# A fused attention and MLP-mixer kernel: another order for its first stage

## The chip, the cores and the metric

The kernel runs on one core of one Trainium2 chip. The time is device time in microseconds (us) of one execution, as the median over several runs. A separate execution is recorded by the hardware profiler; its span runs from the first to the last instruction of the program, and its own time is a little longer than its span, because starting and ending the program lie around it.

The engines are TensorE (PE, matrix products; PEld is its loading of the stationary operand), VectorE (DVE), ScalarE (ACT), GpSimd (POOL) and SyncE (SP), which here issues nearly all loads. Each engine works through its own instructions strictly in the order of the program, and semaphores make it wait for others.

## The reference

Attention without a softmax, for 8 batches of 8 heads, 576 tokens and 64 columns a head, with a root-mean-square normalisation, and then a token and channel mixer on 576 tokens of 512 columns:

```python
kv  = einsum('bhsd,bhse->bhde', k, v)
out = einsum('bhsd,bhde->bhse', q, kv)
rms = sqrt(mean(out * out, axis=-1, keepdims=True) + 1e-6)
x   = out / rms * g_norm                  # heads side by side: (8, 576, 512)
h   = maximum(x.T @ w_tok1, 0) @ w_tok2   # w_tok1 576x256, w_tok2 256x576
u   = x + h.T
out = u + maximum(u @ w_ch1, 0) @ w_ch2   # w_ch1 512x1536, w_ch2 1536x512
```

q, k, v and `g_norm` are float32. The four mixer weights arrive as float64, so the kernel loads their raw 64-bit words and turns them into float32 itself.

## The kernel before

**Tiling.** Batches are taken in pairs. The 576 tokens of a batch are four tiles of 128 rows and a rest of 64; the rests of the two batches of a pair share one tile. For each pair the kernel forms `kv` from k and v (two loads of k and two of v for each batch, half of the columns each), multiplies q by it, normalises, and mixes over tokens. The channel mixer over all batches follows in products of 128x256 and 128x128 blocks, and makes up most of the run. The stage that concerns us is the first: attention of pair 0 (batches 0 and 1), and the first half of its token mixing.

**The order of the work** is written out by hand. Near the end of the main function stand calls that issue loads, and then lists of short names; `play` (line 1192) takes the names one by one and emits the instructions of each. The list of the first stage is `start` (line 1241), the list after it `middle` (line 1247), which works on pair 1's attention and the rest of pair 0's mixing. The names that matter, with a tile number c (0 to 4, where 0 and 1 belong to batch 0, 2 and 3 to batch 1, and 4 is the rest) and a half t of it (128 rows each):

- `kvSH`: k transposed times v on TensorE for batch S, half H of the columns, into a PSUM tile; `eSH` copies it to SBUF as `kvp` (VectorE, line 383, in this stage). `lSH` issues the loads of k and v of the next pair into the same buffers.
- `aCT`: q times `kvp` on TensorE into a PSUM tile `ps_o`, of which there are two. `gCT` multiplies it by `g_norm` into the tile `x` (VectorE, line 444), `qCT` squares it (ScalarE, line 448), `tCT` sums the squares by head (VectorE, line 465).
- `mC`, `rC`, `iC`: mean (VectorE), square root (ScalarE), and a refined reciprocal (four VectorE instructions, lines 479 to 484), for a tile's 256 rows at once.
- The scaling of `x` by the result: `pCT` on GpSimd (`scale_pool`, line 504), `dCT` on VectorE (`scale_vector`, line 500) or `sCT` on ScalarE (line 498, eight instructions).
- `wBK`: turning block B of the raw token weights into float32. `wB0` issues the load; `wB1` is two ScalarE instructions (lines 163 and 166), `wB2`, `wB3`, `wB4` are three of VectorE (lines 169, 173, 178), in that order. Blocks 0 and 1 are the two halves of the columns of `w_tok1`, 2 its last 64 rows, 3 and 4 are `w_tok2`.
- `h0TJ`: the product of row tile J of batch 0's `x` with column block T of `w_tok1`, one matmul of 128x128 by 128x512 into the tile `ps_h` of block T. `h1T` is four such products, of batch 1's `x`.
- `jN`: N matmuls of an identity matrix with itself, whose result nobody reads (`keep_warm`, line 1277).

**Queues.** A load is issued by SP, but v of the first two loads by ScalarE. Loads share eight semaphores in turn, so a load waits until the one eight before it has landed. `load(n)` (line 138) is a load of k and v, `load_q(b)` one of q for a batch, `block[0]()` the load of a raw weight block. Before `start` the order is: `load(0)`, raw blocks 0 and 1, `load(1)`, q of batch 0, `load(2)`, `load(3)`, q of batch 1, and so on.

**Waits by range.** A wait is derived from the range of a tile that an instruction touches, from its first to its last element. `w_tok1` is laid out as rows by 256 columns, so that column blocks 0 and 1 alternate in each partition.

Of the kernel before, what the change touches and what calls it, by code (L numbers as in the profile page):

```python
# [20 lines left out]
def kernel(  # L21
# [90 lines left out]
    def do(f, *a, **kw):  # L112
        return lambda: f(*a, **kw)
# [6 lines left out]
    def dma(o, i, engine=nc.sync):  # L120
        keep(engine.dma_start(o, i))
# [16 lines left out]
    def load(n):  # L138

        if n >= 2 * B:  # L140
            return
        cols = [t[n // 2, :, ts(n % 2, DH)] for t in (k, v)]

        queues = (nc.sync, nc.scalar if n < 2 else nc.sync)
        for dst, c, e in zip((k_in[n % 4], v_in[n % 4]), cols, queues):
            dma(dst[:, :J], c[:LO].rearrange("(j p) e -> p j e", p=P), e)
            dma(dst[:HF, J], c[LO:], e)

    def load_q(b):
        if b < B:  # L150
            qT[b] = qtp.tile([P, HP, LO], F32, name="qT", tag="qT", bufs=2)
            dma(qT[b], q[b].rearrange("(c p) s -> p c s", p=P)[..., :LO])
# [69 lines left out]
    def get_ch2(f):  # L222

        a = 2 * (2 * f // NS)

        def loads(raw):
            t = raw.rearrange("p (h f n) w -> p f h n w", h=2, f=2)
            rows = words(moe_w_ch2)[ts(f, 2 * P)].rearrange("(f p) (h n) w -> f p h n w", f=2, h=2)
            return [(t[:, i], rows[i]) for i in range(2)]

        dst = w_ch2[:, a:a + 2, ds(2 * f % NS, 2)]
        return block(2 * DM, loads, dst.rearrange("p h f n -> p h (f n)"))
# [19 lines left out]
    def t_sums(b):  # L252

        def step(o, x, y):
            return lambda: tensor_add(b(o), b(x), b(y), ALU.subtract)

        return [step(5, 7, 1), step(6, 3, 5), step(7, 3, 7), step(4, 2, 6)]
# [934 lines left out]
    def play(lines, after={}, **stages):  # L1192

        for name in " ".join(lines).split():
            if name.isdigit():
                for _ in range(int(name)):
                    next(stages["rounding"], lambda: None)()
            elif name[0] == "-":  # L1200
                stages["before"][name[1:]]()
            else:
                next(stages[s][name] for s in ("attention", "mixing", "more")
                     if name in stages.get(s, ()))()
# [4 lines left out]
    channel = ([get_ch1(c, f) for f in range(2) for c in range(NC)]  # L1209
               + [get_ch2(f) for f in range(NF // 2)])  # L1210
    load(0)
    for block in tok1[:2]:
        block[0]()
    load(1)
    for t in [t for pair in zip(k_in, v_in) for t in pair]:
        keep(nc.gpsimd.memset(t[HF:, J], 0.0))
    zeroed = [ps["kv"].tile([P, 2, P], F32, name="ps_kv", tag="kv") for _ in range(2)]
    for t in zeroed:
# [5 lines left out]
    make_identity(nc, ident)  # L1224
    dma(g_sb, bass.AP(tensor=g_norm.tensor, offset=g_norm.offset,
                      ap=[[0, P], [0, 1], list(g_norm.ap[0])]), nc.scalar)
    load_q(0)
    for n in range(2, 4):
        load(n)
    load_q(1)  # L1230
# [2 lines left out]
    for block in tok1[2:] + tok2:  # L1233
# [5 lines left out]


    start = [
        "kv00 e00 l00 j14 w01 w11 w02 w03 w04 w12 w13 w14", "kv01 j10 e01 l01",
        "a00 g00 q00", "a01 g01 q01 t00", "a10 g10 q10 t01 m0 r0", "a11 g11 q11 t10 i0 p00 p01",
        "kv10 j6 t11 m1 r1 e10 i1 s10 p11", "kv11 j2 e11", "h000 h001 h002 h003", "a20 g20 q20", "a21 g21 q21 t20",
        "h010 t21 m2 r2", "a30 g30 q30 i2 p20", "a31 g31 q31 t30", "h011 t31 m3 r3 p21", "a40 i3 p30 g40 q40 p31",
        "h012 h013 t40 m4 r4 w21 i4 s40 lq0 l10 l11 lr0 lr1"]
    middle = [
        "kv00 e00 w31 w22 w23 w24", "h10 -lq1 w32 w33 w34", "kv01 e01 w41 w42",
        "h11 w43 w44", "hr l00", "a0 q00 g01 q01 g00 t00 t01", "u0 z2 f0", "u1 l01",
# [20 lines left out]
    more = {f"w{n}{k}": f for n, b in enumerate(tok1 + tok2) for k, f in enumerate(b)}  # L1270
# [6 lines left out]
    def keep_warm(n):  # L1277

        o = ps["h"].tile([P, DM], F32, name="ps_j", tag="h")
        for _ in range(n):  # L1280
            matmul(o[:, :P], lhsT=ident, rhs=ident, start=True, stop=True)

    more |= {f"j{n}": do(keep_warm, n) for n in (2, 6, 10, 14)}
    play(start, attention=attentions[0], mixing=mixings[0], more=more)
    play(middle, attention=attentions[1], mixing=mixings[0], before=attentions[0],
         more=more, rounding=rounding)
    for n in range(1, B // 2 - 1):
        play(steady[n - 1], attention=attentions[n + 1], mixing=mixings[n], before=attentions[n],
             more=more, rounding=rounding)
# [16 lines left out]
    more = {f"c{i}": f for i, f in enumerate(t_sums(lambda n: uT[0][:, SB[n]]))}  # L1306
# [97 lines left out]
```

## Time and profile before

| What | Value |
|---|---|
| Time, median of 3 runs | 789.48 us (788.86 to 789.51) |
| The profiled execution's own time | 788.88 us |
| Its span | 787.1 us |
| PE busy in the span | 774.4 us, 98% |
| VectorE, ScalarE, GpSimd busy | 612.9, 265.4, 78.3 us |
| First matmul starts | 6.24 us |
| First matmul of `middle` starts | 39.79 us |
| DMA from 2 to 79 us | busy throughout, 327 to 351 GB/s by stretch |

A fixed share of time lies outside the span: 788.88 - 787.1 = 1.8 us. TensorE's busy time counts the `jN` matmuls too, and matmuls at a lower clock at their longer duration. In the timeline, a 128x128 float32 matmul is shown as two records, and the `xN` at a line's end counts records.

### The profile page before, as it was taken

The numbers are of one execution on the slowest core, as the hardware profiler recorded it, in microseconds if no ns is written. First come the engines' busy times: TensorE is split into PE (matmuls) and PEld (weight loads), VectorE is DVE, ScalarE is ACT, GpSimd is POOL, SyncE is SP. The second block draws the span as 40 slices with busy tenths as digits, with TensorE's granted clock in tenths as the row PEclk, the third lists the DMA queues.
The fourth block names the chain that finished last, engine by engine and source line by source line (L and its number), as shares of the span: only waits on it lengthen the run. The fifth ranks groups of instructions, "written<-read, shape, count | busy, mean of one in ns | idle before, by whom it ended". The sixth has DMA issues, their size and how long they took to land.

```text
span 787.1 us, 14853 instructions
## 1 busy us (share of the span) xinstructions
PE 774.4 (98%) x5832; PEld 652.6 (83%) x5832; DVE 612.9 (78%) x906; ACT 265.4 (34%) x513; POOL 78.3 (10%) x91
## 2 busy tenths in 40 slices
PE   6999999999999999999999999999999999999998
PEld 5655555544888888999988899998889999889998
DVE  2666887796776868988778889776898885787977
ACT  2356564846110133511133242123352113325211
POOL 1211212122410000010100001010000101000111
PEclk9999999999999999999999999999999999999999
DMA  9999999587699795599897579889559889655864
GB/s 295 327 334 371 361 371 344 212 268 282 235 292 337 269 339 148 154 309 205 246 236 231 151 218 272 247 203 290 148 158 283 206 222 230 200 153 151 200 173 91
DMA packets 132614, 192.12 MB, mean 244 GB/s; under 512 B 13633, under 2 KB 92225, under 8 KB 132545
## 3 DMA queue, kind: packets, MB, share of 16 engines
q1 hardware_dynamic: 115984, 167.54, 68.1%
q0 software_dynamic: 14656, 22.02, 13.7%
q10 hardware_dynamic: 1904, 1.61, 0.7%
q8 instruction: 46, 0.75, 0.4%
q14 instruction: 24, 0.19, 0.1%
HBM read 138.31 MB, written 52.82 MB: 243 GB/s over the span
## 4 chain that ended last, share of the span: by engine, by line
PE 95%; DVE 2%; ACT 1%; DMA 1%; issue 0%; SPq 0%; ACTq 0%
PE ps_d L133 28%; PE ps_b L133 19%; PE ps_a L133 19%; PE ps_h L133 8%; PE ps_u L133 8%; PE ps_v L133 5%; PE ps_c L133 3%; PE ps_kv L133 2%; PE ps_w L133 2%; PE ps_o L133 2%; DMA raw<-in_moe_w_tok_dram 1%; ACT x L498 1%; DVE x L444 0%; DVE ms L465 0%; PE ps_j L133 0%
## 5 line engine op out<-in xcount | busy, mean ns | idle before, releaser
L133 PE MATMUL ps_d<-ui,w 128*128 128x256 f32 x504 | 118.6, 379 | 0.0
L133 PEld LDWEIGHTS ps_d<-ui,w 128*128 128x128 f32 x504 | 95.1, 190 | 12.8 <-DVE v L124 0.2
L130 ACT COPY ps_d<-ps_a 128x768 f32<-128x768 f32 (+1 forms) x56 | 32.0, 571 | 215.6 <-PE ps_a L133 215.6
L124 DVE TENSOR_TENSOR v<-v,v 128x1536 f32<-128x1536 f32 (+2 forms) x70 | 103.5, 1483 | 0.3
L133 PE MATMUL ps_b<-w,sv 128*128 128x128 f32 x672 | 84.7, 276 | 0.0
L133 PE MATMUL ps_a<-w,v 128*128 128x128 f32 x672 | 84.2, 275 | 0.0
L133 PEld LDWEIGHTS ps_a<-w,v 128*128 128x128 f32 x672 | 79.9, 192 | 0.2
L133 PEld LDWEIGHTS ps_b<-w,sv 128*128 128x128 f32 x672 | 79.5, 192 | 0.2
L133 PE MATMUL ps_u<-h,w_tok 128*128 128x512 f32 (+1 forms) x160 | 67.2, 606 | 0.2
L133 PE MATMUL ps_d<-w,v 128*128 128x128 f32 x528 | 66.3, 275 | 0.0
L133 PE MATMUL ps_h<-x,w_tok 128*128 128x512 f32 (+1 forms) x160 | 65.5, 603 | 0.7 <-ACT x L498 0.7
L133 PEld LDWEIGHTS ps_d<-w,v 128*128 128x128 f32 x528 | 62.7, 192 | 0.3
L127 ACT ACTIVATE v<-v 128x768 f32<-128x768 f32 (+1 forms) x54 | 42.6, 821 | 55.1 <-DVE v L124 55.1
L133 PE MATMUL ps_d<-w,sv 128*128 128x128 f32 x480 | 60.1, 275 | 0.0
L133 PEld LDWEIGHTS ps_d<-w,sv 128*128 128x128 f32 x480 | 57.1, 192 | 0.2
L133 PEld LDWEIGHTS ps_h<-x,w_tok 128*128 128x128 f32 (+1 forms) x160 | 26.1, 189 | 32.7 <-issue 29.0
L1121 POOL DMA_DIRECT2D out_dram<-us x11 | 14.1, 1278 | 379.3 <-ACT us L130 347.4
L133 PEld LDWEIGHTS ps_u<-h,w_tok 128*128 128x128 f32 (+1 forms) x160 | 24.8, 179 | 31.0 <-issue 25.6
L133 PE MATMUL ps_a<-uT,w 128*128 128x256 f32 x192 | 46.7, 379 | 0.0
L444 DVE TENSOR_TENSOR x<-ps_o,g_sb 128x512 f32<-128x512 f32 x32 | 21.6, 687 | 28.6 <-PE ps_o L133 23.3
L133 PE MATMUL ps_b<-ui,w 128*128 128x256 f32 x168 | 40.8, 379 | 0.0
L133 PEld LDWEIGHTS ps_a<-uT,w 128*128 128x128 f32 x192 | 36.3, 190 | 4.8
(145 smaller groups left out, 1216.2 us busy)
## 6 DMA issues: line engine op xcount, KB each, us to landing
w<-parts SPq DMA_DIRECT2D x168, 384.0 KB, 4.1
w<-parts SPq DMA_DIRECT2D x56, 192.0 KB, 3.4
uT<-blocks SPq DMA_DIRECT2D x36, 256.0 KB, 5.7
k_in<-in_k_dram SPq DMA_DIRECT2D x16, 512.0 KB, 8.7
qT<-in_q_dram SPq DMA_DIRECT2D x8, 1024.0 KB, 9.2
out_dram<-x POOLq DMA_DIRECT2D x16, 512.0 KB, 6.1
v_in<-in_v_dram SPq DMA_DIRECT2D x14, 512.0 KB, 8.8
raw<-in_moe_w_ch_dram SPq DMA_DIRECT2D x8, 768.0 KB, 10.4
```

The lines of the kernel that those rows point to most:

```text
L124: keep(engine.tensor_tensor(out=o, in0=a, in1=b, op=op))
L127: keep(nc.scalar.activation(o, a, AF.Relu))
L130: keep(nc.scalar.copy(o, a))
L133: keep(nc.tensor.matmul(*a, **kw))
L444: keep(nc.vector.tensor_mul(x, bank[c, h], g_sb.to_broadcast([P, number(c), D])))
L498: keep(nc.scalar.activation(x[:, k, h], x[:, k, h], AF.Copy, scale=inv[:, k, h]))
L1121: keep(nc.gpsimd.dma_start(to.rearrange("t p e -> p t e"), a, accum_op=ALU.add))
```

## The change

In the order of loads, `load(1)` and q of batch 0 go ahead of the raw token weights. In `start`, a long row of identity matmuls comes first, the weights are decoded between the steps of tiles 0 and 1, the `kv` products of batch 1 come between token-mixing products of batch 0, and all scaling that GpSimd did is given to VectorE or ScalarE (`p00 p01 p11 p20 p21 p30 p31` go; of them `d00 d01 d20 d30` are VectorE's and `s11 s21 s31` ScalarE's; `s10` becomes `d10` and `s40` becomes `d40`). The identity matmuls were 14, 10, 6 and 2, and are 24, 8 and 10.

```diff
     load(0)
+    load(1)
+    load_q(0)
     for block in tok1[:2]:
         block[0]()
-    load(1)
...
-    load_q(0)
     for n in range(2, 4):
         load(n)
...
     start = [
-        "kv00 e00 l00 j14 w01 w11 w02 w03 w04 w12 w13 w14", "kv01 j10 e01 l01",
-        "a00 g00 q00", "a01 g01 q01 t00", "a10 g10 q10 t01 m0 r0", "a11 g11 q11 t10 i0 p00 p01",
-        "kv10 j6 t11 m1 r1 e10 i1 s10 p11", "kv11 j2 e11", "h000 h001 h002 h003", "a20 g20 q20", "a21 g21 q21 t20",
-        "h010 t21 m2 r2", "a30 g30 q30 i2 p20", "a31 g31 q31 t30", "h011 t31 m3 r3 p21", "a40 i3 p30 g40 q40 p31",
-        "h012 h013 t40 m4 r4 w21 i4 s40 lq0 l10 l11 lr0 lr1"]
+        "j24 kv00 e00 l00 j8", "kv01 e01 l01", "a00 g00 q00", "a01 g01 q01 t00 t01 m0 w01 r0 w02 w03",
+        "a10 i0 d00 w04 d01 g10 q10 w11", "a11 w12 w13 g11 q11 w14 j10", "h000 h001 t10 t11 m1 r1", "kv10 e10 i1 d10 s11",
+        "h010 h011 kv11 e11", "a20 g20 q20", "a21 g21 q21 t20 t21 m2 r2", "h002 h012", "a30 g30 q30 i2 d20 s21",
+        "h003 h013", "a31 g31 q31 t30 t31 m3 r3", "a40 g40 q40 i3 d30 s31 t40 m4 r4 w21 i4 d40 lq0 l10 l11 lr0 lr1"]
...
-    more |= {f"j{n}": do(keep_warm, n) for n in (2, 6, 10, 14)}
+    more |= {f"j{n}": do(keep_warm, n) for n in (8, 10, 24)}
```

## The prediction

> **What bounds the kernel now.** I read the page first, for the engine that carries the span.
>
> ```profile
> span 787.1 us, 14853 instructions
> ...
> PE 774.4 (98%) x5832; PEld 652.6 (83%) x5832; DVE 612.9 (78%) x906; ACT 265.4 (34%) x513; POOL 78.3 (10%) x91
> ...
> PE 95%; DVE 2%; ACT 1%; DMA 1%; issue 0%; SPq 0%; ACTq 0%
> ```
>
> TensorE is the bound; other engines can stand on the path only where it idles. So second I read whom TensorE waits for:
>
> ```profile
> PE ps_kv L133 <- DMA v_in<-in_v_dram: 6.2, 1, 6.2
> PE ps_kv L133 <- DVE w_tok L178: 1.1, 1, 1.1
> PE ps_o L133 <- ACT sq L448: 0.8, 2, 0.5
> PE ps_h L133 <- ACT x L498: 0.7, 1, 0.7
> PE ps_r L133 <- ACT sq L448: 0.2, 1, 0.2
> ```
>
> Nearly all waits lie before 37 us: asked from 52 us on, the list holds one of 0.2 us. Hence **a delay in the first stage has nothing later to hide in, and a gain nothing that eats it**, as long as loads keep up. (The second row names a decode step; the load of k that this product needs was issued at 6.16 and landed 7.5 us later, at 13.7, when it started. That load is what came last.) Third, TensorE's timeline of the stage:
>
> ```profile
> 6.24 2.40 PE L133 MATMUL ps_kv<-v_in,k_in 128*64 128x64 f32 x40 [6.24 <-DMA v_in<-in_v_dram]
> 8.57 4.07 PE L133 MATMUL ps_j<-ident 128*128 128x128 f32 x28
> 13.77 1.39 PE L133 MATMUL ps_kv<-v_in,k_in 128*64 128x64 f32 x40 [1.14 <-DVE w_tok L178]
> 15.09 2.50 PE L133 MATMUL ps_j<-ident 128*128 128x128 f32 x20
> 17.42 1.95 PE L133 MATMUL ps_o<-kvp,qT 128*128 128x128 f32 x16
> ...
> 23.19 1.60 PE L133 MATMUL ps_j<-ident 128*128 128x128 f32 x12
> ...
> 26.79 1.88 PE L133 MATMUL ps_h<-x,w_tok 128*128 128x512 f32 x4
> ...
> 39.79 1.39 PE L133 MATMUL ps_kv<-v_in,k_in 128*64 128x64 f32 x40
> ```
>
> The stage ends at 39.79, where `middle` begins. Fourth, the single steps on VectorE:
>
> ```profile
> 18.52 0.69 DVE L444 TENSOR_TENSOR x<-ps_o,g_sb 128x512 f32<-128x512 f32 x1 [2.90 <-PE ps_o L133]
> 25.22 0.58 DVE L470 TENSOR_SCALAR ms<-ms 128x16 f32<-128x16 f32 x1
> 61.85 0.69 DVE L502 TENSOR_TENSOR x<-x,inv 128x512 f32<-128x512 f32 x1
> ```
>
> These are a tile's gain, a mean, and a multiply by the reciprocal. The last decode step of weight block 1 ran from 14.37 to 15.06 before, while VectorE had nothing else to do.
>
> **What the Trainium skill says.** "TensorE: Matmul & The Clock Gate", Part 1 (the HAM clock gate): the array runs at half clock until about 4 us of sustained activity, and falls back after an idle window of about 3.4 us. The trace agrees on the first: the same `kv` product takes 2.40 us first and 1.39 later. No run yet shows the second. The same page, Part 2, says that matmuls stay in program order; so one that waits holds up all behind it. "GPSIMD Engine Reference", Specifications: GpSimd shares SBUF interfaces with VectorE; the trace agrees, since the 0.18 us mean took 0.58 at 25.22 while GpSimd multiplied.
>
> **The start.** The identity is ready at 3.4 us, and `j24` needs no load. Warm, a record of it costs (2.50 - 1.60) / 8 = 0.112 us; 48 are 5.4. The slow clock cost 1.0 in the first `kv` (2.40 - 1.39) and 0.7 in `j14` (4.07 against 1.60 + 16 x 0.112), and a little more in matmuls that are cold throughout: 1.8. `j24` ends at 3.4 + 7.2 = 10.6. Then `kv00` (1.3, its next matmul starts 1.3 after it) to 12.0, `j8` (16 records, 1.8) to 13.8, `kv01` to 15.1. Their data are there: v of the first load by 7.0; of the second by 12.0, where it lands today. Then q: now it lands at 7.5 + 9.1 = 16.6; the queue is full, and 1 MB of raw weights goes behind it, 3.1 us at 330 GB/s, so 13.5 to 13.9. It could land anywhere from 13 to 16.6; over 15.1 each us is one lost. I take 13.9, hidden. So `a00` starts at 15.1 (17.42 before), and waits 0.2 inside for `e01`, which nothing now separates from `kv01`. **Gain so far: 2.1 us.**
>
> **The chain to the weights.** Before, a start of `a00` at 17.42 gave the gain at 18.52, the square at 19.24 and so on; the same steps from 15.1, with 0.2 for `e01`:
> - `g00` 16.4, `g01` 17.3, squares to 18.6, sums to 19.35, mean to 19.55.
> - ScalarE does `w01` (two of 0.57) only behind both squares, 18.55 to 19.8, then the root.
> - VectorE: `w02`, `w03` (0.46 each) to 20.35; four steps of the reciprocal (0.96, as 23.68 to 24.64 today) to 21.25; `d00` 0.7, `w04` 0.65, `d01` 0.6, to 23.2.
> - `a10` and `a11` wait for the squares as today and end by 19.6; `j10` (2.2) runs to 21.8. `h000` waits for `w04` and starts at 22.65, 0.85 idle.
> - Block 1: VectorE reaches `g10` after `d01`, to 23.8. On ScalarE `q10` waits for that, and **`w11` stands behind `q10`**: 24.45 to 25.6. VectorE, idle meanwhile, then does `w12`, `w13` (to 26.0), `g11` (to 26.6), `w14` to 27.2.
>
> `h001` reads only block 0. Yet in the built order of the changed kernel `h000` and `h001` each wait for VectorE, while `h010`, which reads block 1, carries no wait. So block 1's end is already waited for, by `h001`; the range rule says the same, as block 1's range covers block 0's columns in rows 1 to 3. `h001` starts at 27.25: TensorE idles 3.7 us after `h000`, with `kv10`, `h010`, `kv11` and all else behind it.
>
> **The rest of the stage.** From 27.25 TensorE has `h001` 0.9, `kv10` 1.3, two products 1.8, `kv11` 1.3, `a20` and `a21` 1.8 with 0.25 for `e11`, then four products 3.6, `a30` and `a31` 1.8, `a40` 1.05: 13.8, so `middle` starts at 41.05. Before had `kv10` and `kv11` done at 26.3. **41.05 - 39.79 = +1.3 us.** That includes what GpSimd's absence returns to VectorE (before, 0.4 to 0.9 us of its chain to `s10`).
>
> **In `middle`**, `h10` needs tiles of batch 1. `a31` ends at 40.2; then `g31`, square, two sums and mean to 42.6, `g40` and the reciprocal to 44.1, `d30` to 44.8. `kv00` and two products reach 44.2: 0.7 idle. `s31` (ScalarE, eight in 2.02) follows from 44.13 to 46.15; the product before it ends at 45.9: 0.4. Before: no wait there. **+1.2 us.** GpSimd's seven multiplies (1.04 each) lay off the path; VectorE's five single ones are in the sums above.
>
> **Loads.** Bytes to 16.6 us are the same. Pair 1's second load of v lands at 29.7 + 7.4 = 37.1, before 41.05. Its buffers are read at the latest by `kv11`, at 32.6; the reload into them is issued from 40.0 on. No load becomes late.
>
> Sum: +1.3 + 1.2 = **+2.5 us**. The profiled execution took 788.88 = 787.1 + 1.8, so 791.4 on it; its time is 0.6 below the median of 789.48, and on the median it is **792.0 us**. A change under about 0.2% (1.6 us) can't be told from none.
>
> **Rivals.**
> - *`h001` does not wait for block 1* (not slower, 0.14). Then `h001` and `kv10` (2.2 us) run in the gap, and `h010` waits at 27.25: +0.3, 789.8. For it: the product reads block 0 alone. Against: the built waits. It decides at `w14` done by about 25: earlier, the change gains.
> - *TensorE's clock falls back in the gap* (slower, 0.22). From 21.8 to 27.25 it works 0.9 us; if that counts as idle, 3.4 us (the page's window) at half speed cost, as an estimate, 1.7: +4.2, 793.7. For it: 3.7 us is more than the window; against: the window has to lie wholly in the gap.
> - *q or the decode is later than taken* (0.06), by 1 to 1.5 us: q at 16.6 gives +4.0, 793.5.
> - That the change doesn't do what it says is out: the built order shows loads, decodes and GpSimd's multiplies where the diff puts them.
>
> **Numbers.** The forecast has 0.58; its own range is +1.3 to +3.9, for 0.5 either way in the ramp of the clock, 0.7 in the chain and 0.5 in `middle`. It gives 0.51 of slower; the second and third rivals 0.28: 0.79 slower, 0.17 within 0.2%, 0.04 faster, mostly the first rival's spread. The range leaves out a tenth each side: 790.3 (+0.8) to 794.6 (+5.1).
>
> **What would show it.** The first `kv` near 10.6; `ps_o` near 15.1; one `ps_h` matmul near 22.65 and a gap of 3 to 4 us up to the end of the second L178; a ScalarE decode behind a square near 24.5; `middle` from 41; two short waits in it. Longer `kv` after the gap (2.4, not 1.4) means the fallback. It is wrong if the second `ps_h` follows the first at once, or if `middle` starts before 40.

## The result, and the profile after

| What | Before | After |
|---|---|---|
| Median of the runs made together | 789.40 us (788.86 to 789.88, 6 runs) | 794.28 us (793.58 to 795.27, 6 runs) |
| Ratio to before, 95% interval | | 1.0065 (1.0052 to 1.0078) |
| The profiled execution's time and span | 788.88, 787.1 us | 794.29, 792.5 us |
| First matmul of `middle` | 39.79 us | 43.10 us |
| First `ps_u` product, further on in `middle` | 52.69 us | 57.26 us |

The changed kernel is slower by 4.9 us on the medians and by 5.4 us between the two profiled executions. Of the 5.4 us, 4.6 are lost before the first `ps_u` product (57.26 - 52.69), so the place to read is the first 57 us. (`ps_u` is the PSUM tile of the mixer's second matrix product.)

From the page of the changed kernel: span, busy times, and the shares of the chain that ended last.

```profile
span 792.5 us, 14890 instructions
...
PE 779.5 (98%) x5852; PEld 656.4 (83%) x5852; DVE 616.1 (78%) x912; ACT 267.0 (34%) x521; POOL 71.3 (9%) x84
...
PE 92%; DMA 4%; ACT 1%; DVE 1%; issue 0%; ACTq 0%; SPq 0%
```

TensorE is still the bound at 98%, yet it is *busy* for 5.1 us longer (779.5 against 774.4) with only 20 records more, which at 0.11 us each would be 2.2 us. Some of its work took longer. The 4% of DMA in the chain are for the most part no late loads: 24.8 us of it (3.1%) are loads before 27.71, reached only because one wait that ends there is put down to a q load, wrongly, as shown next. Experiment 1 has the same loads, and its chain has PE 96% and no DMA. Whom TensorE waits for (total, number of waits, longest, in us):

```profile
PE ps_j L133 <- POOL ident masks.py:199: 3.5, 1, 3.5
PE ps_h L133 <- DMA qR<-in_q_dram: 3.4, 1, 3.4
PE ps_o L133 <- ACT sq L448: 0.8, 2, 0.5
PE ps_h L133 <- DVE x L502: 0.6, 1, 0.6
PE ps_d L133 <- DVE v L124: 0.6, 1, 0.6
PE ps_h L133 <- DVE w_tok L178: 0.5, 1, 0.5
PE ps_h L133 <- ACT x L498: 0.2, 1, 0.2
```

The wait of 6.2 us for the first v has become one of 3.5 for the identity matrix, and one of 3.4 us has appeared in front of a `ps_h` product. It carries the name of a q load. TensorE's timeline (start, duration, what, and in brackets the idle time before and what ended it) shows when it ended:

```profile
3.48 7.67 PE L133 MATMUL ps_j<-ident 128*128 128x128 f32 x48 [3.48 <-POOL ident masks.py:199]
11.07 1.39 PE L133 MATMUL ps_kv<-v_in,k_in 128*64 128x64 f32 x40
...
15.69 2.20 PE L133 MATMUL ps_o<-kvp,qT 128*128 128x128 f32 x16
...
23.21 1.12 PE L133 MATMUL ps_h<-x,w_tok 128*128 128x512 f32 x2 [0.52 <-DVE w_tok L178]
27.71 1.55 PE L133 MATMUL ps_h<-x,w_tok 128*128 128x512 f32 x2 [3.38 <-DMA qR<-in_q_dram]
29.19 2.40 PE L133 MATMUL ps_kv<-v_in,k_in 128*64 128x64 f32 x40
...
33.51 1.39 PE L133 MATMUL ps_kv<-v_in,k_in 128*64 128x64 f32 x40
...
43.10 1.33 PE L133 MATMUL ps_kv<-v_in,k_in 128*64 128x64 f32 x40
```

and the timelines of VectorE and ScalarE show what was being done in that gap:

```profile
23.68 0.68 DVE L444 TENSOR_TENSOR x<-ps_o,g_sb 128x512 f32<-128x512 f32 x1
25.57 0.43 DVE L169 TENSOR_SCALAR w_tok<-w_tok 128x512 f32<-128x512 f32 x1 [1.21 <-ACT w_tok L163]
...
26.98 0.68 DVE L178 CUSTOM_DVE_ANT_1 w_tok<-w_tok,raw 128x1024 uint16<-128x1024 uint16 x1
```

```profile
24.39 0.60 ACT L448 ACTIVATE sq<-ps_o 128x512 f32<-128x512 f32 x1 [3.92 <-DVE x L444]
24.89 0.65 ACT L163 ACTIVATE w_tok<-raw 128x512 f32<-128x512 f32 x1
```

The last decode step of weight block 1 ends at 26.98 + 0.68 = 27.66, and `h001` starts at 27.71: the decode ended the wait, not the q load that is named. ScalarE idles 3.92 us in front of tile 1's square at 24.39, with `w11` (24.89) queued behind it; so block 1 is decoded only after that, while VectorE in turn idles 1.21 us.

The second thing to see is the length of two `kv` products of 40 records: 2.40 us at 29.19, right after the gap, and 1.39 at 33.51. The table by windows says why. Its columns are the window, its length, busy time of PE, PEld, DVE, ACT and POOL (with instructions), TensorE's granted clock (1.00 is full speed), DMA share, GB/s:

```profile
24.86:28.27 3.41, 0.56 (x2) 0.30 (x2) 2.67 (x6) 1.83 (x4) 0.00 (x0) 1.00 1.16 300
28.28:31.69 3.41, 3.41 (x43) 2.38 (x41) 0.79 (x3) 0.21 (x1) 0.00 (x0) 0.50 1.02 320
31.69:35.10 3.41, 3.41 (x46) 2.10 (x47) 1.99 (x7) 2.02 (x8) 0.00 (x0) 1.00 1.08 331
```

After 3.41 us in which TensorE was busy for 0.56, the clock is granted at one half for 3.41 us, to the hundredth from 28.28 to 31.69, and then in full again. This is the second rival of the prediction.

### The profile page after: what moved, and what is told of

The parts are those of the page before. It is cut to its first block, busy times and chain, and to the rows that moved or that the text cites. A ratio compares the mean times of both kernels' runs of the same rounds, so it can differ in the third digit from the quotient of the medians.

```text
span 792.5 us, 14890 instructions
## 1 busy us (share of the span) xinstructions
PE 779.5 (98%) x5852; PEld 656.4 (83%) x5852; DVE 616.1 (78%) x912; ACT 267.0 (34%) x521; POOL 71.3 (9%) x84
## 4 chain that ended last, share of the span: by engine, by line
PE 92%; DMA 4%; ACT 1%; DVE 1%; issue 0%; ACTq 0%; SPq 0%
PE ps_d L133 27%; PE ps_b L133 18%; PE ps_a L133 18%; PE ps_u L133 8%; PE ps_h L133 8%; PE ps_v L133 5%; PE ps_c L133 3%; DMA v_in<-in_v_dram 2%; PE ps_kv L133 2%; PE ps_w L133 2%; PE ps_o L133 2%; ACT x L498 1%; DMA qR<-in_q_dram 1%; DMA xt<-out_dram 1%; DMA w<-parts 1%
## 5 line engine op out<-in xcount | busy, mean ns | idle before, releaser
L133 PEld LDWEIGHTS ps_d<-ui,w 128*128 128x128 f32 x504 | 95.1, 190 | 13.6 <-DVE v L124 1.0
L133 PEld LDWEIGHTS ps_u<-h,w_tok 128*128 128x128 f32 (+1 forms) x160 | 24.8, 179 | 31.0 <-issue 25.9
```

The costliest lines, as they stand in the source:

```text
L133: keep(nc.tensor.matmul(*a, **kw))
```

## The experiments

Each is a whole kernel, run with a profile and timed beside runs of the kernel before on the same chip, whose medians were 789.15 us (24 runs; the first four experiments) and 789.00 us (27 runs; the others). "To `ps_u`" is how much later the first `ps_u` product starts than before, in the profiled execution; "clock" says whether the profiled execution shows a fallback after the start, that is, a stretch in which the clock is granted at one half.

| Experiment | Median us | Ratio (95%) | Span against 787.1 | To `ps_u` | Clock falls back |
|---|---|---|---|---|---|
| changed kernel | 794.28 | 1.0065 (1.0052 to 1.0078) | +5.4 | +4.6 | yes |
| 1 gap filled | 791.95 | 1.0038 (1.0026 to 1.0050) | +2.8 | +2.8 | no |
| 2 decode earlier | 790.49 | 1.0021 (1.0013 to 1.0029) | +1.7 | +1.6 | no |
| 3 `kv10` in the gap | 792.42 | 1.0045 (1.0033 to 1.0057) | +3.8 | +3.2 | yes |
| 4 GpSimd scales | 791.40 | 1.0040 (1.0026 to 1.0054) | +2.1 | +1.7 | no |
| 5 old loads, new order | 795.60 | 1.0078 (1.0065 to 1.0091) | +6.2 | +5.9 | yes |
| 6 new loads, old order | 792.77 | 1.0040 (1.0027 to 1.0053) | +3.5 | +3.3 | yes |
| 7 shorter rows of identities | 792.97 | 1.0042 (1.0030 to 1.0054) | +2.8 | +2.8 | yes |
| 8 put together | 787.76 | 0.9983 (0.9976 to 0.9990) | -1.8 | -1.9 | no |

### 1. The gap filled with matmuls that nobody reads

```diff
-"h000 h001 t10 t11 m1 r1"
+"h000 k14 h001 t10 t11 m1 r1"
```

`k14` is 14 more identity matmuls, written into the tile that `j10` wrote. The wait for block 1 stays; only TensorE's idleness goes.

> The changed kernel with 14 identity matmuls between the first and the second token-mixing product, where TensorE idled 3.4 us; nothing else moves. If the idle stretch made the clock fall back (half speed for 3.4 us after it), the granted clock stays full, the kv product behind the gap takes 1.4 us instead of 2.4, the middle list starts about 1.6 us earlier (41.5 instead of 43.1) and the kernel is about 3.3 us slower than before instead of 4.9. If the slow clock has another cause, or costs nothing on the path, the time stays at +4.9. The second product still starts at 27.2 to 27.7, because its wait is untouched.

Measured: 791.95 us, +2.8. TensorE's timeline of this kernel, and its window on the same place:

```profile
23.94 3.29 PE L133 MATMUL ps_j<-ident 128*128 128x128 f32 x28
27.48 1.13 PE L133 MATMUL ps_h<-x,w_tok 128*128 128x512 f32 x2 [0.26 <-DVE w_tok L178]
28.54 1.39 PE L133 MATMUL ps_kv<-v_in,k_in 128*64 128x64 f32 x40
...
41.36 1.33 PE L133 MATMUL ps_kv<-v_in,k_in 128*64 128x64 f32 x40
```

```profile
24.35:27.76 3.41, 3.15 (x27) 2.96 (x27) 2.38 (x5) 2.14 (x4) 0.00 (x0) 1.00 1.15 332
27.76:31.20 3.44, 3.44 (x45) 1.94 (x45) 2.16 (x8) 0.22 (x1) 0.00 (x0) 1.00 1.06 263
```

`h001` still starts when the decode ends. But `kv10` takes 1.39 us, the clock stays whole, and from `h001` to `middle` it is 41.36 - 27.48 = 13.9 us, where the changed kernel took 43.10 - 27.71 = 15.4. Work that computes nothing makes the kernel 2.1 us faster (+4.9 against +2.8, each against the runs of the kernel before made beside it). So this much of the loss hangs on TensorE's idleness in the gap. The half clock itself can take 1.7 us of it at most (3.41 us at one half). Between the two traces (2.6 us of span) 1.5 us lie between `h001` and `middle`, 0.2 in the start, where full clock came at 7.28 us and not at 7.80, and 0.9 behind the first `ps_u`, where the changed kernel's trace has a wait of 0.57 us at 291 us and this one has none. The +2.8 left is what the order of the work costs, and it is close to the forecast sum of +2.5.

### 2. Block 1 decoded ahead of tile 1's gain and square

```diff
-"a10 i0 d00 w04 d01 g10 q10 w11", "a11 w12 w13 g11 q11 w14 j10"
+"a10 i0 d00 w04 w11 d01 w12 w13 w14 g10 q10", "a11 g11 q11 j10"
```

> The changed kernel with the decode of weight block 1 ahead of tile 1's gain and square on VectorE and ScalarE. If the decode queued behind that square is what holds the second token-mixing product, the last decode step ends near 25.2 instead of 27.7, the idle stretch shrinks to about 1 us, the clock stays full, the middle list starts near 39.1, and the kernel is 0.5 to 1.2 us slower than before (the two waits in the middle list stay). If VectorE's having taken over GpSimd's multiplies is the cause, the work of VectorE is the same and the time stays above +3 us.

Measured: 790.49 us, +1.3, a little over the upper end that was expected. TensorE's timeline:

```profile
16.26 2.20 PE L133 MATMUL ps_o<-kvp,qT 128*128 128x128 f32 x16
...
23.79 1.12 PE L133 MATMUL ps_h<-x,w_tok 128*128 128x512 f32 x2 [0.52 <-DVE w_tok L178]
26.23 1.13 PE L133 MATMUL ps_h<-x,w_tok 128*128 128x512 f32 x2 [1.32 <-DVE w_tok L178]
```

The gap shrinks from 3.38 to 1.32 us, by moving nothing but ScalarE's and VectorE's steps of block 1. `h001` moved with them, to the end of block 1's last step (25.48 + 0.69 = 26.17), though block 0 had been ready since 23.73: the product of column block 0 does wait for column block 1, as its range in the layout makes it. What is left of its +1.6 to `ps_u` is 0.3 at the start of `middle` (40.11 against 39.79) and 1.3 in it.

This kernel also bears on the price of the clock, without any edit. Of its 18 runs, five had a mean granted clock of 0.998 and took 792.45 to 793.10 us; the 13 at 1.0 took 789.44 to 791.10. A fallback of 3.41 us at one half takes 1.7 us of clock from 790, which is 0.2%, so a mean of 0.998 is about one such period. No trace of these five runs was kept, so where the period lay is not shown. The medians of the two groups (792.55 and 790.23) differ by 2.3 us, about what filling the gap gave.

### 3. `kv10` moved into the gap

```diff
-"h000 h001 t10 t11 m1 r1", "kv10 e10 i1 d10 s11"
+"h000 kv10 h001 t10 t11 m1 r1", "e10 i1 d10 s11"
```

> The changed kernel with the kv product of batch 1's first half put into the gap, between the first and the second token-mixing product (its loads have landed by 21.9). The second product's wait is untouched, so it starts at 27.3 to 27.7 as before; 1.3 us of work leave the path and, if a gap of about 2 us no longer lets the clock fall back, 1.6 us of slow clock too: middle list from about 40.2, time about +2.0 us over before. If only the order of the products counts and the clock falls back anyhow, +3.6.

Measured: 792.42 us, +3.3: the case in which the clock falls back anyway. TensorE's timeline and windows:

```profile
24.24 1.39 PE L133 MATMUL ps_kv<-v_in,k_in 128*64 128x64 f32 x40
27.70 4.54 PE L133 MATMUL ps_h<-x,w_tok 128*128 128x512 f32 x6 [2.08 <-DVE w_tok L178]
32.17 1.39 PE L133 MATMUL ps_kv<-v_in,k_in 128*64 128x64 f32 x40
```

```profile
24.78:28.19 3.41, 1.33 (x31) 1.00 (x27) 2.60 (x6) 1.90 (x4) 0.00 (x0) 1.00 1.17 313
28.19:31.60 3.41, 3.41 (x5) 1.35 (x4) 2.64 (x9) 1.50 (x7) 0.00 (x0) 0.50 1.00 303
```

No idle stretch is longer than 2.08 us here, and the clock still falls back, in all five runs (0.998 or 0.997). TensorE was busy 1.33 of the 3.41 us, 39%. Moving real work into the gap gains 1.6 us (+4.9 against +3.3), about the 1.3 us of the product and a little more, but it doesn't save the clock. That idleness must span a whole window was my reading, and it falls.

### 4. GpSimd scales again where it did

```diff
-"a10 i0 d00 w04 d01 g10 q10 w11"
+"a10 i0 p00 w04 p01 g10 q10 w11"
...
-"kv10 e10 i1 d10 s11"
+"kv10 e10 i1 s10 p11"
...
-"a30 g30 q30 i2 d20 s21"
+"a30 g30 q30 i2 p20 p21"
...
-"a40 g40 q40 i3 d30 s31 t40 m4 r4 w21 i4 d40 ..."
+"a40 g40 q40 i3 p30 p31 t40 m4 r4 w21 i4 s40 ..."
```

> The changed kernel with GpSimd's multiplies back where they were (p00, p01, p11, p20, p21, p30, p31, and ScalarE's s10 and s40), loads, decodes and products in the changed order. If the load that VectorE took over is the cause of the slowdown, nearly all of it goes: within 0.8 us of before. If the place of the decode is the cause, only the two multiplies ahead of the second block's decode leave VectorE's chain: the second product starts about 1.3 us earlier, near 26.4, the idle stretch is about 2.6 us, the clock probably stays full, and the time is +1.5 to +2.5 us; GpSimd slows VectorE's small steps meanwhile and can take some of that back.

Measured: 791.40 us, +2.3. TensorE's timeline:

```profile
15.64 2.20 PE L133 MATMUL ps_o<-kvp,qT 128*128 128x128 f32 x16
...
23.28 1.12 PE L133 MATMUL ps_h<-x,w_tok 128*128 128x512 f32 x2 [0.63 <-POOL x L506]
26.38 1.10 PE L133 MATMUL ps_h<-x,w_tok 128*128 128x512 f32 x2 [1.97 <-DVE w_tok L178]
```

VectorE without `d00` and `d01` reaches tile 1's gain 1.4 us sooner (22.25 against 23.68), so block 1 is ready at 26.23, not 27.66, and in four of six runs the clock doesn't fall back. That is the saving; between the medians it is 0.6 us against the filled gap of experiment 1, where the clock was whole too. The delay of `h001` is better counted from the first q product (`a00`), which leaves the start out: 27.71 - 15.69 = 12.02 us in the changed kernel, 26.38 - 15.64 = 10.74 here, 26.23 - 16.26 = 9.97 in experiment 2. So the scaling on VectorE delays `h001` by 1.3 us and the place of the decode by 2.1, the larger of the two; both undone in one kernel was not run, so they are not to be added.

The Trainium skill ("GPSIMD Engine Reference", Specifications) says that GpSimd shares SBUF interfaces with VectorE, and that they contend when a VectorE step has two SBUF inputs or runs in a mode that uses two ports. From 21.87 to 24.22 GpSimd multiplied here, and the decode step (0.63 us, two SBUF inputs) and the gain (0.68, one of its inputs in PSUM) beside it took no longer than the 0.69 and 0.68 of the changed kernel. What was slowed to 0.58 in the kernel before was a step of 128x16 elements, and here one of 128x8 took 0.57 us at 43.75 beside GpSimd, against 0.17 at 47.50 in the changed kernel. When a step is slowed and when not stays open.

### 5 and 6. The two halves of the change alone

Experiment 5 has the new `start` with the old order of loads, experiment 6 the old `start` with the new order of loads:

```diff
     load(0)
-    load(1)
-    load_q(0)
     for block in tok1[:2]:
         block[0]()
+    load(1)
...
+    load_q(0)
     for n in range(2, 4):
```

> The changed order of steps with the order of loads of before (raw weights ahead of the second load of k and of q). q then lands near 16.6 again instead of 13.6, so the q product starts at 16.6 to 16.8 instead of 15.7 and everything behind it is 1.0 us later: about +6 us over before. If the order of loads is itself what slows the changed kernel, it gets faster instead, towards before.

> The order of steps of before with the changed order of loads (q and the second load ahead of the raw weights), GpSimd's multiplies included. In that order the decode of both weight blocks stands on VectorE ahead of the second copy of kv, which the q product needs; the second raw block now lands near 18.0, so its decode ends near 20.6, the q product gets past its first half only at 21 (17.4 before), and the kernel is 3 to 4 us slower than before. If loads alone gain, it is 1 to 3 us faster. It shows that the new order of loads asks for a later decode.

Measured: 795.60 us (+6.6) and 792.77 us (+3.8). TensorE's timeline of experiment 5, then of experiment 6:

```profile
17.30 2.02 PE L133 MATMUL ps_o<-kvp,qT 128*128 128x128 f32 x16 [1.25 <-DMA qT<-in_q_dram]
...
29.14 2.07 PE L133 MATMUL ps_h<-x,w_tok 128*128 128x512 f32 x2 [3.38 <-DVE w_tok L178]
```

```profile
16.56 0.61 PE L133 MATMUL ps_o<-kvp,qT 128*128 128x128 f32 x4
20.21 5.06 PE L133 MATMUL ps_o<-kvp,qT 128*128 128x128 f32 x28 [3.04 <-DVE kvp L383]
```

With the old loads q arrives 1.25 us after TensorE could use it, and the first product starts at 17.30, not 15.69. Of these 1.6 us 0.3 were lost before, to the start's clock (`kv01` starts at 14.66, not 14.37); so the new order of loads gains about 1.3 us inside the new `start`. With the old `start`, the same loads do harm: the decode steps stand ahead of `e01` on VectorE, the raw weights now arrive later, and TensorE waits 3.04 us for the copied `kvp`. There too the clock falls back after the gap (28 records take 5.06 us, where 16 took 1.95 at full clock before), in the trace at least: one of the four runs had a mean clock of 1.0 and took 791.30 us. Neither half is good alone, and both together (+4.9) are no better than the new loads alone (+3.8).

### 7. Shorter rows of identity matmuls

```diff
-"j24 kv00 e00 l00 j8", "kv01 e01 l01"
+"j12 kv00 e00 l00 j4", "kv01 e01 l01 j6"
```

> The changed kernel with identity matmuls cut ahead of q: 12 and 4 instead of 24 and 8, and 6 between the second kv product and q, so that each kv product starts near the landing of its loads and the q product at 13.7, when q has landed, instead of 15.7. If the identity matmuls hold the head of the chain, the whole stage is 1.5 to 2 us earlier (middle list near 41.3) and the kernel is +3 over before. If something else holds it (the loads or the decode's raw words, landing at 15.1 and 18.0), it stays at +4.9.

Measured: 792.97 us, +4.0; the profiled execution alone, 791.67 us, is +2.8 on the span. TensorE's timeline:

```profile
14.10 1.95 PE L133 MATMUL ps_o<-kvp,qT 128*128 128x128 f32 x16
...
25.87 1.90 PE L133 MATMUL ps_h<-x,w_tok 128*128 128x512 f32 x2 [3.37 <-DVE w_tok L178]
```

The identity matmuls stood in the way: q has landed by 13.6, and the first product starts at 14.10, 1.6 us sooner than in the changed kernel. The wait of 3.37 us and the fallback stay, so this doesn't show what the gap costs. Three of the five runs had a mean clock of 0.996, which would be two periods at one half. Two of the changed kernel's six runs had it too, and took 795.21 and 795.27 us, about 1 us more than the others. None of these five runs has a trace, so where the second period lies is open. It doesn't explain why the median gained less than the profiled execution: the two runs here at 0.998 took 791.67 and 792.97 us.

### 8. What was learned, put together

Short rows of identities, block 1 decoded early, `kv10` in the gap, some of tile 2 to 4's steps earlier, tile 3 scaled by VectorE alone, and the raw blocks of `w_tok2` issued from within `start`, behind the next pair's k and v:

```diff
-    for block in tok1[2:] + tok2:
+    for block in tok1[2:]:
...
+        "j12 kv00 e00 l00 j4", "kv01 e01 l01 w30 w40 j6", "a00 g00 q00", "a01 g01 q01 t00 t01 m0 w01 r0 w02 w03",
+        "a10 i0 d00 w04 w11 d01 w12 w13 w14 g10 q10", "a11 g11 q11 j8", "h000 kv10 h001 t10 t11 m1 r1", "e10 i1 d10 s11",
+        "h010 h011 kv11 e11 h002", "a20 g20 q20", "a21 g21 q21 t20 t21 m2 r2", "h012 a30 g30 q30 i2 d20 s21",
+        "a31 g31 q31 t30 t31 m3 r3 i3 d30 d31", "h003 h013 a40 g40 q40 t40 m4 r4 w21 i4 d40 lq0 l10 l11 lr0 lr1"]
```

> Everything learned in one version: fewer identity matmuls ahead of q (12, 4, 6), the decode of block 1 ahead of tile 1's gain and square, the kv product of batch 1 in the gap, the two w_tok2 blocks loaded after pair 1's k and v, tile 3 scaled by VectorE alone, and products moved between the q products of batch 1 so that none waits. By the same steps as in the prediction the middle list starts near 36.5 to 38.5 (39.8 before; pair 1's loads land near 35), one wait of about 1 us stays in it, the clock stays full, and the kernel is 1 to 3 us faster than before. If loads bound the stage anyway, it is within 0.8 us of before.

Measured over 22 runs: 787.76 us, 1.2 us faster than the kernel before (ratio 0.9983, 0.9976 to 0.9990). TensorE's timeline:

```profile
14.12 2.02 PE L133 MATMUL ps_o<-kvp,qT 128*128 128x128 f32 x16
...
22.53 1.39 PE L133 MATMUL ps_kv<-v_in,k_in 128*64 128x64 f32 x40
23.92 2.84 PE L133 MATMUL ps_h<-x,w_tok 128*128 128x512 f32 x6
...
36.83 1.33 PE L133 MATMUL ps_kv<-v_in,k_in 128*64 128x64 f32 x40
```

The block-1 wait is gone: `kv10` covers it, `h001` and what follows run at once, and 3.0 us of the stage are saved (36.83 against 39.79), of which a wait of 0.81 us in `middle` gives some back. One of the 22 runs had a mean clock of 0.997 and took 791.46 us. So an order with most parts of the change can pay when the decode of block 1 does not stand in two queues behind tile 1. How much each edit of this kernel gives was not taken apart, and the later loads of `w_tok2`, which are no part of the change, were not tried in the kernel before.

## Why the prediction was right and wrong

It named the slower side, its reason, and a range (790.3 to 794.6) that holds 794.28. But the +4.9 lie outside the forecast's own range, +1.3 to +3.9; the whole range reaches so far only because it takes in the rivals, and one came true to which the prediction gave 0.22 and against which it argued. The likeliest number, 792.0, was 2.3 us low. Step by step, in the profiled execution:

- **The start.** `j24` was to end at 10.6 and `a00` to start at 15.1; they did at 11.07 and 15.69. The mechanism held (loads and q hidden, q landed at 13.6), the size of the slow clock was short by 0.5: `j24`'s 48 records took 7.67 us against 5.4 in full clock, 2.3 us lost where 1.8 were taken from the kernel before. By the trace's clock records full speed came at 7.80 us here and at 7.28 to 10.50 in the experiments. The Trainium skill says the same in "TensorE: Matmul & The Clock Gate", Part 1: activity is counted in a window that runs freely, so the same kernel meets it in different phases.
- **The chain to the weights.** `h000` 23.21 (22.65) and `h001` 27.71 (27.25) are late by that half microsecond and no more; the idle gap was 3.38 (3.7). ScalarE's decode behind the square started at 24.89 (24.45). Right, and that `h001` waits for block 1 was shown by experiment 2, so the first rival falls.
- **The rest of the stage.** Forecast 13.8 us, measured 15.4. *This is the step that failed.* It was costed at full clock. Experiment 1, at full clock, took 13.9.
- **The argument against the second rival**, "the window has to lie wholly in the gap", was wrong. Window and half speed follow the same page's figure (3.41 us measured, the page says about 3.4), but its picture of an idle window, which I took to mean wholly idle, does not fit: 0.56 us of work in it (changed kernel) and 1.33 us (experiment 3) did not count as busy enough. The measurement decides. The rival's price, 1.7 us as an estimate, was 1.5 us between `h001` and `middle`, and 2.1 to 2.3 us between medians.
- **In `middle`.** The two waits came where they were put: 0.58 us on VectorE's scaling (0.7 forecast) and 0.20 on ScalarE's (0.4). But from the first `h10` matmul to the next `kv` it took 49.30 - 44.36 = 4.94 us against 44.73 - 41.10 = 3.63 before, 1.3 us, so each wait cost some 0.26 us beyond its idle time. The eight matmul records were busy for 1.98 + 1.12 + 1.12 = 4.22 us in three groups, where they took 3.70 in one row before. The sum forecast (1.2) was right by luck: its own two terms, 0.7 and 0.4, make 1.1, and both were too long. Nor does this loss hang on which engine scales. With the scaling back on GpSimd (experiment 4) the same passage took 46.40 - 41.49 = 4.91 us. VectorE took six single multiplies, not the five of the prediction; the sixth, `d40` at 49.20, held nothing up here.
- **Loads.** Pair 1's second load of v was to land at 37.1; it landed by 38.5, before 43.10. None was late in this stage. At 291 us a wait of 0.57 appears (`ps_d` for `v`, listed above); VectorE had waited 3.32 us for a load of `xt` until 286.6. Experiments 3 and 4 show 0.4 and 0.2 of it, the others and the kernel before none. What delays that load stays open.

Sum by the first `ps_u`: 2.5 forecast + 0.5 (start) + 1.5 (clock) + 0.1 (`middle`) = 4.6, as measured.

## What to carry to other kernels

A gap on TensorE can have two prices: its length, and a period at half clock behind it. To judge the second, don't ask whether one idle stretch is long enough, but how busy TensorE is around it within 3.41 us; 39% of a window was too little. Where the windows fall is not set by the program: in experiment 4 the stretch from 22.97 to 26.38 us has TensorE busy for only 1.13 us (33%), but it lay across two windows, and the clock of that trace stayed whole. In two of that kernel's six runs the clock fell back. And when a step is moved for one consumer, look for who else waits on the range it writes, and what stands before it in the other engine's queue.

## What the runs showed of the hardware

- In every trace with a fallback after the start (the changed kernel and experiments 3, 5, 6 and 7) the half clock lasts 3.41 us, and follows a window of 3.41 us with TensorE busy for 0.56, 1.33, 0.31, 0.53 and 0.21 us. The clock keeps to a grid of such windows: between coming up and falling back, the full clock lasts 20.48 us in the changed kernel and experiments 3 and 5, 17.07 in 7 and 10.24 in 6, which is six, five and three times 3.413. Experiments 2 and 4 had windows with 1.75 and 1.79 us and kept the full clock. Their windows are counted on from where full clock came, at 8.99 and 7.69 us. The table by windows of experiment 2, then of experiment 4:

```profile
22.64:26.05 3.41, 1.75 (x8) 0.73 (x6) 3.11 (x6) 1.25 (x2) 0.00 (x0) 1.00 1.07 337
26.05:29.46 3.41, 3.23 (x44) 2.03 (x45) 3.31 (x8) 1.41 (x3) 0.00 (x0) 1.00 1.14 270
```

```profile
24.76:28.17 3.41, 1.79 (x28) 1.06 (x30) 2.83 (x6) 0.81 (x2) 0.00 (x0) 1.00 1.14 316
```

So the bound lies between 1.33 and 1.75 of 3.41 us (39% and 51%), as far as busy time is what counts. It is not the number of matmul records: 31 in experiment 3's window were too few, 8 in experiment 2's were enough. Nor is it the time of the weight loads, 1.00 us against 0.73. Whether it is busy time itself, no run here tells. The way up is another matter: in experiment 2 TensorE works without a break from 3.48 us, and the window from 2.16 to 5.57 has it busy for 2.09 us (61%), yet full clock came only after the next, at 8.99.

- The windows' phase against the program differs between the traces: with the same row of identities first, full clock came at 7.28 to 8.99 us. So a kernel close to that bound can have two times. Experiment 2 was 2.3 us slower in 5 of 18 runs, those with the lower mean clock; that the phase is the reason is inferred. Single runs of such a kernel can't be compared at the level of 0.2%.
